# Hash attention followed by a gated feed-forward network: one pair of heads hashed together, and row loads, clears and squares moved in the order of work

## The chip, the cores and the metric

The kernel runs on one core of a Trainium2 chip. A core has a matrix engine (PE, TensorE; its weight loads are listed as PEld), a vector engine (DVE, VectorE), an activation engine (ACT, ScalarE), a general engine (POOL, GpSimd) and a queue engine (SP, SyncE), which work side by side and wait for each other by semaphores. Sixteen DMA engines move data between the chip's memory and the on-chip buffer; transfers are issued by SP, ACT or POOL. The metric is the device time of one execution in microseconds. The kernel before takes 329.41 us (median of three runs, 329.21 to 329.52).

## The reference

Attention over 4 batches, 8 heads, 768 positions of 64 values, in which a query sees only the keys of its own hash bucket, then a gated network over the 3072 rows that result.

```python
q_bits = (np.einsum('bhsd,dk->bhsk', q, proj) > 0)      # 6 bits a position, k the same
mask = q_bucket[:, :, :, None] == k_bucket[:, :, None, :]
scores = np.where(mask, scale * q @ k.T, -1e9)
attn = exp(scores - max);  attn /= (sum(attn) + 1e-9)
x = (attn @ v)  -> [3072, 512]
xn = x / sqrt(mean(x*x) + 1e-6) * rms_g
out = (silu(xn @ w_gate) * (xn @ w_val)) @ w_out        # 512 -> 1536 -> 512
```

## The kernel before, in words

**Tiling.** A batch is cut in two halves of 384 queries: `w` = 0 to 7 counts them over the batches. A *slot* is one score tile: a half `w`, a head `h` and a third `p` of the keys, two matmuls of 128 keys by 384 queries (`scores`, L355), followed by one exponential on ACT (`probs`, L365). The list `SLOTS` fixes their order. The first ones are: slots 0 to 5 are heads 0 and 1 (pair 0) for `w` = 0, slots 6 to 11 the same pair for `w` = 1, slots 12 to 17 pair 1 for `w` = 0, 18 to 23 pair 2, 24 to 29 pair 3, and from 30 on the other pairs for `w` = 1.

**Hash bits as rows.** The mask is not computed by itself. A score operand in `QK` holds the 64 values of q or k and, below them, 12 rows of hash bits, scaled so that a matmul over 76 rows gives a usable score only where all bits agree. There are six `QK` buffers, used in turn by the pairs of heads. For some pairs the matmul runs over all 128 rows instead; for them the rows below the bits must be zero (`clear_rows`, L139).

**From rows to scores.** A pair's q and k come by one load each (`load_rows`, L117, on SP). PE turns them (`turn_pe`, L181), DVE or ACT copies the result from PSUM (`keep`, L189), and POOL or ACT writes it to `QK` as 16-bit values (`cast_half`, L195 and L197). PE multiplies the turned values with the projection (`hash_bank`, L221), DVE makes bits of the signs (L228), and these are moved to their rows of `QK`. `hash_head` hashes one head, twice over, so that each block of bits has a strip of its own; three of the four blocks are then copied by DVE (L261) and one by an SP transfer (L259). `hash_heads` hashes both heads of a pair in the same four matmuls: four blocks are copied by DVE (L281) and four go by SP transfers (L279). Before, heads 2 and 3 use the first way, pairs 2 and 3 of batch 0 and the pairs of batch 1 the second.

**After the scores.** `av` (L377) multiplies the exponentials with v for a pair of heads into one PSUM tile `o_ps`, of which there is one buffer. `attn_out` empties it on DVE (`otmp`, L392, and a reciprocal, L397). `attn_x` multiplies by the reciprocal (`x`, L404) and squares (`sq`, L416), on POOL for all pairs but two; `sumsq` reduces the squares on DVE (L420). When a half's four pairs are through, `norm` makes the row scale (L427 on DVE, L429 and L433 on POOL), `scale_x` and `turn_x` make the operand of the network (L444, L458), whose matmuls (`gate` L473, `value` L483, `project` L496) are spread over the slots of the next half.

**What sets the order.** The order is written out by hand. `at(slot, function, ..., rank=)` puts a step into a slot's list, and the last loop goes through the slots: first the scores of the next slot, then the steps of rank under 3, then the exponential, then the rest by rank and by the order in which they were put. Every engine, and the DMA queues of SP and POOL, runs its own instructions in this order and waits at the first that is not ready. The loads of weights (`load_w`, L549) are issued by POOL, two halves for each of the two matrices.

The row loads of batch 1 stand in slots 9, 11 and 13 (k, q, v of pair 0) and 13, 14 and 36 (pair 1). The bits of pair 2 are moved by SP from slot 12 on.

Of the kernel before, what the change touches and what calls it, by code (L numbers as in the profile page):

```python
# [8 lines left out]
FP32 = mybir.dt.float32  # L9
# [7 lines left out]
S = 768  # L17
D = 64
# [3 lines left out]
HALF = 384  # L22
# [26 lines left out]
def kernel(  # L49
# [33 lines left out]
    pk = const.tile([128, 48], FP32, name="pk")  # L83
    pq = const.tile([128, 48], FP32, name="pq")
    thr = const.tile([128, 1], FP32, name="thr")
    scl = const.tile([128, 1], FP32, name="scl")
    mhalf = const.tile([128, 3], FP32, name="mhalf")
    gcol = const.tile([128, 4], FP32, name="gcol")
# [46 lines left out]
        if (b, hp) not in QK:  # L135
            QK[b, hp] = qkbuf[len(QK) % len(qkbuf)]

    def clear_rows(i):
        nc.gpsimd.memset(qkbuf[i][D:128].rearrange("p h n -> p (h n)").bitcast(FP32), 0.0)  # L139

    def score_rows(b, hp):
        return slice(0, 128 if (b, hp) in ((1, 0), (1, 1)) or b > 1 else KROWS)

    def t_tile(b, hp, which):
        T0[b, hp, which] = tpool.tile(
# [97 lines left out]
    def hash_head(h):  # L243


        kt, qt = t0(0, h, "k"), t0(0, h, "q")
        ps = hash_bank(
            [(pk[:, 0:32], kt), (pq[:, 0:32], qt), (pk[:, 12:44], kt), (pq[:, 12:44], qt)]
        )
        bt = bits_tile(h)  # L250
        signs(bt, ps)

        def move(movers, t0=0):
            for t, eng in enumerate(movers, t0):
                src = bt[32 * t : 32 * t + 12]
                if eng is nc.scalar:
                    nc.scalar.copy(bit_rows(0, h, t), src)
                elif eng is nc.sync:
                    eng.dma_start(out=bit_rows(0, h, t), in_=src)  # L259
                else:  # L260
                    eng.tensor_copy(bit_rows(0, h, t), src)  # L261

        return move
# [81 lines left out]
    def idle(ps, n):  # L345

        for _ in range(n):
            nc.tensor.matmul(ps, ones16, ones16, start=True, stop=True)  # L348

    def scores(g):  # L350
        w, h, p = SLOTS[g]
        ps = scps.tile([128, 2, 512], FP32, name="s_ps")
        idle(ps[:, 0, HALF:512], {0: 8, 3: 6}.get(g, 0))
        for j in range(2):
            nc.tensor.matmul(  # L355
                ps[:, j, 0:HALF], k_cols(w // 2, h, 2 * p + j), q_cols(w, h),
                start=True, stop=True,
            )
        sps[g] = ps
# [25 lines left out]
    def attn_out(w, hp):  # L385
        b = w // 2
        if w not in x:
            x[w] = xpool.tile([128, 3, DMODEL], FP32, name="x")
            ssp[w] = xpool.tile([128, 3, 4], FP32, name="ssp")
        o = ot.pop((w, hp))  # L390
        tmp = spool.tile([128, 3, 2, 66], FP32, name="otmp")
        nc.vector.tensor_add(  # L392
            tmp[:, :, :, 0:65], o[:, :, :, 0:65],
            cvb[b % 2][:, 2 * hp : 2 * hp + 2, 0:65].unsqueeze(1).to_broadcast([128, 3, 2, 65]),
        )
        r = spool.tile([128, 3, 2, 1], FP32, name="rcp")
        nc.vector.reciprocal(r, tmp[:, :, :, 64:65])  # L397
        return tmp, r

    def attn_x(w, hp, tmp, r):  # L400
        xd = x[w][:, :, 128 * hp : 128 * hp + 128]
        urgent = (w, hp) in ((0, 2), (0, 3))
        eng = nc.vector if urgent else nc.gpsimd
        eng.tensor_mul(  # L404
            xd.rearrange("p c (h d) -> p c h d", h=2), tmp[:, :, :, 0:64],
            r.to_broadcast([128, 3, 2, 64]),
        )
        sq = spool.tile([128, 3, 128], FP32, name="sq")
        if urgent:
            for c in range(3):  # L410
                nc.vector.scalar_tensor_tensor(
                    out=sq[:, c], in0=xd[:, c], scalar=1.0, in1=xd[:, c],
                    op0=ALU.mult, op1=ALU.mult, accum_out=ssp[w][:, c, hp : hp + 1],
                )
        else:
            nc.gpsimd.tensor_mul(sq, xd, xd)  # L416
        return sq
# [97 lines left out]
        load_rows(nc.sync, 0, hp, which)  # L515

    nc.vector.memset(ones16, 1.0)
    make_identity(nc, ident)
    nc.gpsimd.dma_start(out=pn[64:128], in_=proj)
    nc.vector.memset(pm, 0.0)  # L520
# [21 lines left out]
    for i in range(2):  # L542
        nc.gpsimd.memset(vls[i][:, :, :, 64:65], 1.0)
        nc.gpsimd.memset(vsum[i][:, :, 64:65], 6.0)
    clear_rows(4)
    clear_rows(5)

    def load_w(dst, src, n0, n1):
        nc.gpsimd.dma_start(  # L549
# [15 lines left out]
    def columns_of_proj():  # L565
        rows = pn.unsqueeze(1).to_broadcast([128, 4, 6])
        for t, sign in ((pk, 1.0), (pq, -1.0)):
            nc.vector.scalar_tensor_tensor(
                out=t[:, 0:24].rearrange("p (c n) -> p c n", n=6), in0=pm, scalar=sign,
                in1=rows, op0=ALU.mult, op1=ALU.mult,  # L570
            )
# [11 lines left out]
    keep(nc.scalar, 0, 0, "q")  # L583
    cast_half(0, 0, "q", 0, nc.scalar)
    columns_of_proj()
    idle(wz[:, 0:128], 5)
    bits0 = hash_head(0)
    keep(nc.scalar, 0, 1, "k")
# [23 lines left out]

    moves = {}

    def hash_one(h):
        moves[h] = hash_head(h)
        moves[h]((nc.sync,), 3)

    def hash_pair(b, hp):
        moves[b, hp] = hash_heads(b, hp)  # L620
        odd = [(0, 2), (1, 2), (0, 3), (1, 3)]
# [2 lines left out]

    for h in range(2):
        at(1 + h, cast_half, 0, h, "q", 1)
        at(h, (bits0, bits1)[h], (nc.vector,), 3)

    for hp, turns, sv in ((1, (1, 2, 3, 5), 8), (2, (7, 8, 9, 10), 17), (3, (12, 13, 14, 15), 22)):
        for i, s in enumerate(turns):  # L630
            at(s, keep_pair, 0, hp, i)
            at(s + 1, casts, 0, hp, i)
            if i % 2:
                at(s + 2, cast_half, 0, 2 * hp + i // 2, "q", 0, nc.scalar)
        at(sv, v_prep, 0, hp)

    for h, s in ((2, 4), (3, 7)):
        at(s, hash_one, h)
        for t in range(3):
            at(s + 1 + t, lambda h=h, t=t: moves[h]((nc.vector,), t), rank=5)  # L640
    for hp, s, slots in ((2, 12, (13, 14, 15, 16)), (3, 17, (18, 19, 20, 21))):
        at(s, hash_pair, 0, hp)
        for i, s in enumerate(slots):
            at(s, lambda hp=hp, i=i: moves[0, hp](nc.vector, [divmod(i, 2)]), rank=5)
    for hp, s in enumerate((6, 16, 22, 30)):
        at(s, v_mean, 0, hp, 2, range(6))
    for i, (t, src) in enumerate(((wg, moe_w_gate), (wv, moe_w_val))):
        at(2 + 4 * i, load_w, t, src, 0, 768)
        at(19 + 5 * i, load_w, t, src, 768, 1536)
        at(38 + 7 * i, load_wo, 6 * i, 6 * i + 6)  # L650

    at(78, load_grow)


    for hp, loads, turns, sh, evens, sv in (
        (0, (9, 11, 13), (20, 21, 24, 27), 33, (41, 42), (27, 44)),
        (1, (13, 14, 36), (29, 31, 33, 35), 40, (45, 47), (49, 51)),
    ):
        for which, sl in zip("kqv", loads):
            at(sl, load_rows, nc.sync, 1, hp, which)  # L660
        for i, sl in enumerate(turns):
            at(sl, keep_pair, 1, hp, i)
            at(sl + 1, casts, 1, hp, i)
        at(sh, hash_pair, 1, hp)
        for hh, sl in enumerate(evens):
            at(sl, cast_half, 1, 2 * hp + hh, "q", 0)
        at(sv[0], v_prep, 1, hp)
        at(sv[1], v_sum, 1, hp)
# [30 lines left out]
    for hp, s in enumerate((48, 62, 64, 78)):  # L699
        at(s, v_mean, 1, hp, 2)  # L700

    for i, s in ((2, 76), (3, 78), (0, 97), (1, 98)):
        at(s, clear_rows, i, rank=6)

    gts, sqs = {}, {}
# [20 lines left out]
    for w in range(8):  # L726
        for h in range(H):
            end = LAST[w, h] + (2 if (w, h) == (0, 7) else 3)
            at(end - 1, av, w, h, 0, 9)
            at(end, av, w, h, 9, 18)  # L730
            if h % 2:
                if (w, h) == (1, 1):
                    at(end, o_first, w, 0, rank=4.5)
                    at(end + 3, o_last, w, 0, rank=4.5)
                else:
                    at(end, o_step, w, h // 2, rank=4.5)
                if (w, h) not in ((0, 5), (0, 7)):
                    late = 3 if h == 7 and w < 7 else 4
                    at(end + late, s_step, w, h // 2, rank=5)
        s0 = 24 * w + 42  # L740
        n0 = {0: 11, 2: 7, 3: 13, 4: 13, 5: 13, 6: 13}.get(w, 11)
        at(s0 - n0, norm, w, rank=5)
        for c in range(3):
            scale, rank = {0: 6, 2: 6 - c}.get(w, 8 - c), 1
            turn = {0: (4, 3, 2), 2: (4, 2, 1)}.get(w, (5, 3, 1))[c]
            if w in BY_DMA and c < 2:
                scale, turn, rank = 11 - c, 11 - c, 6
            at(s0 - scale, scale_x, w, c, rank=5)
            at(s0 - turn, turn_x, w, c, rank=rank)
        seen = set()  # L750
        for ft in range(NF):
            for f, s in ((g_step, s0 + 16 * ft // NF), (v_step, s0 + (32 * ft + 16) // (2 * NF))):
                at(s, f, w, ft, rank=4 if s in seen else 2)
                seen.add(s)
        for i in range(9 if w < 7 else 6):
            c, j = divmod(i, 3)
            at(s0 + 16 + i, project, w, c, 4 * j, 4 * j + 4, rank=1 if i == 8 else 3)
# [55 lines left out]
```

## Time and profile before

| | |
|---|---|
| median of three runs | 329.41 us |
| the profiled execution's own time | 329.47 us |
| its span (first to last instruction) | 327.6 us |
| granted TensorE clock, mean | 0.998 |
| read from memory, written to it | 28.58 MB, 6.29 MB |
| SP's transfers, share of 16 DMA engines over the span | 35.2% |
| POOL's transfers, the same | 9.3% |

Rows of a timeline give the start and the time in us, the engine, the line, what is written and read, and in brackets the idle time before, with what ended it. A "q" behind an engine's name is its instruction queue, which issues transfers. The chain is the work that ended last, followed back from the last instruction.

### The profile page before, as it was taken

What the parts mean: (1) busy time and instruction counts of PE and PEld (TensorE: products, weight loads), DVE (VectorE), ACT (ScalarE), POOL (GpSimd) and SP (SyncE); (2) the same over time, 40 slices, a digit from 0 to 9 for tenths busy, and PEclk for the clock granted to TensorE, in tenths of its full rate; (3) what the DMA queues carried; (4) which work ended last, traced back from release to release, by engine and by line L of the source; (5) the groups of instructions that cost most, each with busy time, mean ns of one, the idle gap of its engine ahead of it and who ended that gap; (6) DMA issues with size and microseconds to landing.
All of it is one profiled execution on the core that took longest, in us unless ns stands there. A gap on an engine that the chain in (4) does not pass through costs nothing.

```text
span 327.6 us, 7853 instructions
## 1 busy us (share of the span) xinstructions
PE 321.5 (98%) x2975; PEld 199.5 (61%) x2975; DVE 234.9 (72%) x526; ACT 208.1 (64%) x324; POOL 165.4 (50%) x238
## 2 busy tenths in 40 slices
PE   8998999999999999999999999999999999999995
PEld 7576766655566556655566656566566656655654
DVE  4798896888598976989487865967267824793860
ACT  3788986775576666657576766667677766423331
POOL 7887977278658685686734274733221320230000
PEclk9999999999999999999999999999999999999999
DMA  7998988984359729911470814001200012002002
GB/s 216 358 212 244 165 131 154 151 179 70 119 109 172 128 48 226 155 39 26 130 128 18 150 24 152 3 18 22 78 32 2 11 24 98 0 3 96 2 0 97
DMA packets 85509, 32.69 MB, mean 100 GB/s; under 512 B 70376, under 2 KB 82400, under 8 KB 85472
## 3 DMA queue, kind: packets, MB, share of 16 engines
q1 hardware_dynamic: 81392, 27.28, 35.2%
q0 software_dynamic: 3712, 4.72, 9.3%
q8 instruction: 23, 0.38, 0.5%
q10 hardware_dynamic: 368, 0.20, 0.2%
q14 instruction: 14, 0.11, 0.1%
HBM read 28.58 MB, written 6.29 MB: 106 GB/s over the span
## 4 chain that ended last, share of the span: by engine, by line
PE 94%; DMA 2%; ACT 2%; DVE 0%; issue 0%; DVEq 0%; ACTq 0%
PE v_ps L483 19%; PE s_ps L355 19%; PE y_ps L496 18%; PE g_ps L473 15%; PE o_ps L377 10%; PE d_ps L221 4%; PE s_ps L473 4%; PE t_ps L181 2%; DMA QK<-bits 2%; ACT psb L365 1%; PE z_ps L348 1%; PE x_ps L458 1%; DMA out_dram<-ysb 1%; PE m_ps L336 1%; DVE bits L228 0%
## 5 line engine op out<-in xcount | busy, mean ns | idle before, releaser
L365 ACT ACTIVATE psb<-s_ps 128x768 f16<-128x768 f32 x192 | 150.7, 809 | 30.1 <-PE s_ps L355 28.1
L355 PE MATMUL s_ps<-QK 128*128 128x384 f16 (+1 forms) x384 | 93.7, 326 | 1.3 <-DMA QK<-bits 0.5
L483 PE MATMUL v_ps<-xnT,wv 128*128 128x384 f16 x384 | 78.1, 326 | 0.0
L496 PE MATMUL y_ps<-wo,ht 128*128 128x512 f16 x276 | 69.2, 379 | 0.0
L404 POOL TENSOR_TENSOR x<-otmp,rcp 128x384 f32<-128x384 f32 x30 | 25.7, 857 | 83.4 <-DVE rcp L397 83.2
L377 PEld LDWEIGHTS <-psb 128*128 128x128 f16 x1152 | 51.7, 98 | 21.8 <-issue 3.7
L475 ACT ACTIVATE t<-g_ps 128x384 f32<-128x384 f32 x78 | 38.2, 490 | 40.7 <-PE g_ps L473 38.2
L473 PE MATMUL g_ps<-xnT,wg 128*128 128x384 f16 x312 | 63.5, 326 | 0.0
L484 DVE SCALAR_TENSOR_TENSOR t<-t,g_ps 128x384 f32<-128x384 f32 x78 | 42.9, 550 | 28.3 <-ACT t L475 28.2
L485 DVE SCALAR_TENSOR_TENSOR ht<-t,v_ps 128x384 f16<-128x384 f32 x96 | 53.2, 554 | 11.5 <-PE v_ps L483 1.0
L377 PE MATMUL o_ps<-vl,psb 128*128 128x65 f16 x1152 | 56.0, 193 | 0.0
L483 PEld LDWEIGHTS <-wv 128*128 128x128 f16 x384 | 36.5, 98 | 22.9
L473 PEld LDWEIGHTS <-wg 128*128 128x128 f16 x384 | 36.1, 98 | 23.0
L496 PEld LDWEIGHTS <-ht 128*128 128x128 f16 x276 | 26.3, 98 | 26.5 <-issue 2.1
L355 PEld LDWEIGHTS <-QK 128*128 128x128 f16 (+1 forms) x384 | 31.1, 97 | 16.8 <-issue 3.1
L503 ACT COPY ysb<-y_ps 128x512 f32<-128x512 f32 x23 | 13.5, 585 | 24.3 <-PE y_ps L496 23.7
L392 DVE TENSOR_TENSOR otmp<-o_ps,cvb 128x390 f32<-128x390 f32 x32 | 17.9, 559 | 14.9 <-PE o_ps L377 14.8
L416 POOL TENSOR_TENSOR sq<-x 128x384 f32<-128x384 f32 x30 | 25.5, 849 | 2.4
L213 POOL CAST QK<-kT 64x768 f16<-64x768 f32 x20 | 17.0, 848 | 10.8 <-DVE kT L205 8.9
L213 POOL CAST QK<-qT 64x768 f16<-64x768 f32 x20 | 16.5, 823 | 10.8 <-DVE qT L205 8.1
L205 DVE STREAM_TRANSPOSE kT<-kL 128x192 f32<-128x192 f32 x40 | 19.7, 521 | 0.0
L205 DVE STREAM_TRANSPOSE qT<-qL 128x192 f32<-128x192 f32 x40 | 19.4, 518 | 0.0
(81 smaller groups left out, 307.2 us busy)
## 6 DMA issues: line engine op xcount, KB each, us to landing
vL<-in_v_dram SPq DMA_DIRECT2D x16, 384.0 KB
out_dram<-ysb SPq DMA_DIRECT2D x23, 256.0 KB
kL<-in_k_dram SPq DMA_DIRECT2D x40, 96.0 KB
qL<-in_q_dram SPq DMA_DIRECT2D x40, 96.0 KB
kL<-in_k_dram SPq DMA_DIRECT2D x5, 384.0 KB
qL<-in_q_dram SPq DMA_DIRECT2D x5, 384.0 KB
wg<-in_moe_w_gate_dram POOLq DMA_DIRECT2D x2, 768.0 KB, 8.5
wv<-in_moe_w_val_dram POOLq DMA_DIRECT2D x2, 768.0 KB, 9.6
```

The costliest lines, as they stand in the source:

```text
L205: nc.vector.transpose(dst.rearrange("p (c t r) -> p r c t", c=6, r=4)[:, r : r + 1], src.rearrange("p (r c) d -> p r c d", r=4)[:, r : r + 1],
L213: nc.gpsimd.tensor_copy(QK[b, hp][0:64, hh, o : o + S], T0[b, hp, which][64 * hh : 64 * hh + 64, :])
L355: nc.tensor.matmul(ps[:, j, 0:HALF], k_cols(w // 2, h, 2 * p + j), q_cols(w, h), start=True, stop=True,)
L365: nc.scalar.activation(psb[w, h][:, p], sps.pop(g)[:, :, 0:HALF], AF.Exp, scale=ESCALE,)
L377: nc.tensor.matmul(o[:, c, hh, 0:65], psb[w, h][:, jt // 2, jt % 2, 128 * c : 128 * c + 128], vls[b % 2][:, h, v_chunk(b, h, jt), 0:65], s ...
L404: eng.tensor_mul(xd.rearrange("p c (h d) -> p c h d", h=2), tmp[:, :, :, 0:64], r.to_broadcast([128, 3, 2, 64]),)
L473: nc.tensor.matmul(g, wg[:, kt, fs], xnT[w][:, kt], start=(kt == 0), stop=(kt == 3))
L475: nc.scalar.activation(t, g, AF.Tanh, scale=0.5)
L483: nc.tensor.matmul(vv, wv[:, kt, fs], xnT[w][:, kt], start=(kt == 0), stop=(kt == 3))
L484: nc.vector.scalar_tensor_tensor(out=t, in0=t, scalar=1.0, in1=g, op0=ALU.add, op1=ALU.mult)
L485: nc.vector.scalar_tensor_tensor(out=ht[w][:, ft], in0=t, scalar=0.5, in1=vv, op0=ALU.mult, op1=ALU.mult)
L496: nc.tensor.matmul(y, ht[w][:, ft, c * 128 : (c + 1) * 128], wo[:, ft, :], start=(ft == 0), stop=(ft == NF - 1),)
```

## The change

- `hash_one` is gone. Heads 2 and 3 are hashed as a pair by `hash_heads` at slot 5; the four even blocks are copied by DVE at slots 6, 7, 9 and 10, the other four go by SP. Before, head 2 was hashed at slot 4 and head 3 at slot 7.
- The turns of that pair stand at slots 1, 1, 2 and 3 (before 1, 2, 3 and 5), with their casts one slot, and ACT's casts two slots, behind.
- The last bit blocks of heads 0 and 1 are copied at slots 2 and 4, at the end of the slot.
- The six idle matmuls ahead of slot 3's scores are gone.
- Clears: POOL clears buffers 1 and 2 at the start, ACT buffer 4 (a copy of a zero column), DVE buffer 5 in two halves. Later POOL clears buffer 0 at slot 50 and 3 at slot 78 (before: 2, 3, 0 and 1 at 76, 78, 97 and 98). More pairs use all 128 rows.
- Row loads of batch 1: slots 6, 6 and 9 for pair 0, slots 9, 9 and 36 for pair 1.
- x and squares of pair 0: `attn_out` stays at the end of the pair for `w` = 0 and 1, but `attn_x` goes to slots 22 and 24 and `sumsq` to slots 24 and 26 (before: `attn_x` at slots 8 and 17, `sumsq` at 12 and 18). The reduce of pair 1 for `w` = 0 goes from slot 24 to 22. `otmp` and `rcp` get three buffers, `sq` one.
- The second halves of the gate and value weights are issued at slots 21 and 25 (before 19 and 24).
- Pair 2's even blocks are copied at slots 13, 13, 15 and 16 (before 13 to 16).

```diff
-    def clear_rows(i):
-        nc.gpsimd.memset(qkbuf[i][D:128].rearrange("p h n -> p (h n)").bitcast(FP32), 0.0)
+    def clear_rows(i, eng=nc.gpsimd, heads=(0, 1)):
+        for h in (heads if eng is nc.vector else (0,)):
+            part = qkbuf[i][D:128, h] if eng is nc.vector else (
+                qkbuf[i][D:128].rearrange("p h n -> p (h n)"))
+            part = part.bitcast(FP32)
+            if eng is nc.scalar:
+                eng.copy(part, zcol[D:128].to_broadcast([D, 2 * S]))
+            else:
+                eng.memset(part, 0.0)
 
     def score_rows(b, hp):
-        return slice(0, 128 if (b, hp) in ((1, 0), (1, 1)) or b > 1 else KROWS)
+        return slice(0, KROWS if (b, hp) in ((0, 0), (0, 3)) else 128)
...
-        idle(ps[:, 0, HALF:512], {0: 8, 3: 6}.get(g, 0))
+        idle(ps[:, 0, HALF:512], {0: 8}.get(g, 0))
...
-        tmp = spool.tile([128, 3, 2, 66], FP32, name="otmp")
+        tmp = spool.tile([128, 3, 2, 66], FP32, name="otmp", bufs=3)
...
-        sq = spool.tile([128, 3, 128], FP32, name="sq")
+        sq = spool.tile([128, 3, 128], FP32, name="sq", bufs=1)
...
-    clear_rows(4)
-    clear_rows(5)
+    clear_rows(1)
+    clear_rows(2)
+    clear_rows(4, nc.scalar)
+    clear_rows(5, nc.vector, (0,))
...
     columns_of_proj()
+    clear_rows(5, nc.vector, (1,))
...
     for h in range(2):
         at(1 + h, cast_half, 0, h, "q", 1)
-        at(h, (bits0, bits1)[h], (nc.vector,), 3)
+        at(2 + 2 * h, (bits0, bits1)[h], (nc.vector,), 3, rank=6)
 
-    for hp, turns, sv in ((1, (1, 2, 3, 5), 8), (2, (7, 8, 9, 10), 17), (3, (12, 13, 14, 15), 22)):
+    for hp, turns, sv in ((1, (1, 1, 2, 3), 8), (2, (7, 8, 9, 10), 17), (3, (12, 13, 14, 15), 22)):
...
-    for h, s in ((2, 4), (3, 7)):
-        at(s, hash_one, h)
-        for t in range(3):
-            at(s + 1 + t, lambda h=h, t=t: moves[h]((nc.vector,), t), rank=5)
-    for hp, s, slots in ((2, 12, (13, 14, 15, 16)), (3, 17, (18, 19, 20, 21))):
+    for hp, s, slots in (
+        (1, 5, (6, 7, 9, 10)), (2, 12, (13, 13, 15, 16)), (3, 17, (18, 19, 20, 21))
+    ):
         at(s, hash_pair, 0, hp)
...
-        at(19 + 5 * i, load_w, t, src, 768, 1536)
+        at(21 + 4 * i, load_w, t, src, 768, 1536)
...
-        (0, (9, 11, 13), (20, 21, 24, 27), 33, (41, 42), (27, 44)),
-        (1, (13, 14, 36), (29, 31, 33, 35), 40, (45, 47), (49, 51)),
+        (0, (6, 6, 9), (20, 21, 24, 27), 33, (41, 42), (27, 44)),
+        (1, (9, 9, 36), (29, 31, 33, 35), 40, (45, 47), (49, 51)),
...
-    for i, s in ((2, 76), (3, 78), (0, 97), (1, 98)):
+    for i, s in ((0, 50), (3, 78)):
         at(s, clear_rows, i, rank=6)
...
             if h % 2:
-                if (w, h) == (1, 1):
+                if w < 2 and h == 1:
                     at(end, o_first, w, 0, rank=4.5)
-                    at(end + 3, o_last, w, 0, rank=4.5)
+                    at(22 + 2 * w, o_last, w, 0, rank=4.5)
+                    at(24 + 2 * w, s_step, w, 0, rank=4)
                 else:
                     at(end, o_step, w, h // 2, rank=4.5)
-                if (w, h) not in ((0, 5), (0, 7)):
+                if (w, h) not in ((0, 1), (0, 5), (0, 7), (1, 1)):
                     late = 3 if h == 7 and w < 7 else 4
-                    at(end + late, s_step, w, h // 2, rank=5)
+                    if (w, h) == (0, 3):
+                        at(22, s_step, w, 1, rank=4)
+                    else:
+                        at(end + late, s_step, w, h // 2, rank=5)
```

More of the change, by code (lines that the diff above doesn't have):

```diff
@@ L85 @@
     thr = const.tile([128, 1], FP32, name="thr")
+    zcol = const.tile([128, 1], FP32, name="zcol")
     scl = const.tile([128, 1], FP32, name="scl")
@@ L395, in attn_out @@
         )
-        r = spool.tile([128, 3, 2, 1], FP32, name="rcp")
+        r = spool.tile([128, 3, 2, 1], FP32, name="rcp", bufs=3)
         nc.vector.reciprocal(r, tmp[:, :, :, 64:65])
@@ L517 @@
     nc.vector.memset(ones16, 1.0)
+    nc.vector.memset(zcol, 0.0)
     make_identity(nc, ident)
@@ L613 @@
     moves = {}
-    def hash_one(h):
-        moves[h] = hash_head(h)
-        moves[h]((nc.sync,), 3)
     def hash_pair(b, hp):
```

## The prediction, made before the result was known

> **What bounds the kernel now.** I read the page first (busy shares, then the chain that ended last), then who waited for whom on the tensor engine, then the timelines of its first 50 us, since every edit lies there.
>
> ```profile
> span 327.6 us, 7853 instructions
> PE 321.5 (98%) x2975; PEld 199.5 (61%) x2975; DVE 234.9 (72%) x526; ACT 208.1 (64%) x324; POOL 165.4 (50%) x238
> ...
> PE 94%; DMA 2%; ACT 2%; DVE 0%; issue 0%; DVEq 0%; ACTq 0%
> ```
>
> ```profile
> PE s_ps L355 <- DMA QK<-bits: 0.5, 1, 0.5
> ```
>
> TensorE (PE) is 94% of the chain, and its longest wait after the start is 0.5 us, for one transfer: its program is the time. So an edit counts for what it takes out of PE's list, or for a wait that it puts into it. The one transfer in the chain is the move of hash bits into the score operand.
>
> ```profile
> 4.01 0.85 PE L181 MATMUL t_ps<-ident,kL 128*128 128x128 f32 x3
> 4.66 0.85 PE L181 MATMUL t_ps<-ident,qL 128*128 128x128 f32 x3
> ...
> 10.97 0.50 PE L348 MATMUL s_ps<-ones 128*128 128x128 f16 x6 [0.24 <-ACT psb L365]
> 11.30 0.49 PE L355 MATMUL s_ps<-QK 76*128 76x384 f16 x2
> ...
> 20.93 0.49 PE L355 MATMUL s_ps<-QK 76*128 76x384 f16 x2
> ...
> 28.83 0.65 PE L355 MATMUL s_ps<-QK 76*128 76x384 f16 x3 [0.47 <-DMA QK<-bits]
> ...
> 30.37 0.49 PE L181 MATMUL t_ps<-ident,kL 128*128 128x128 f32 x3
> 30.70 0.44 PE L377 MATMUL o_ps<-vl,psb 128*128 128x65 f16 x9
> ...
> 36.50 0.44 PE L377 MATMUL o_ps<-vl,psb 128*128 128x65 f16 x9
> ```
>
> These are PE's own rows (start, time): two sets of transposes at the start, the six idle matmuls of slot 3, the scores of slot 13, the second half of slot 19's scores (waiting for the bits of pair 2), the last AV of pair 1 (slot 20), and the first AV of head 6 (slot 28). A slot is one score tile.
>
> **The change, part by part.**
>
> *PE work that goes.* Heads 2 and 3 were hashed one by one, and are now hashed as one pair; the six idle matmuls go.
>
> ```profile
> 13.17 1.00 PE d_ps L221 x8
> ...
> 16.81 0.78 PE d_ps L221 x8
> ...
> 22.78 0.68 DVE bits L228
> 23.48 5.21 DMA QK<-bits
> ```
>
> In the chain the hash of head 2 starts at 13.17 and that of head 3 at 16.81; one of them, 0.78 us, goes. The idle matmuls fill 10.97 to 11.30, 0.33 us, behind a wait of 0.24 us that ends earlier when a transpose stands there instead. PE gains 0.78 + 0.33 + 0.24 = 1.35 us up to slot 12.
>
> *The bits of pair 1* now go by four transfers of SP, not two; one is needed at slot 13 (before: VectorE wrote it). The pair's hash stands one slot later than head 2's did, so its bits are ready at about 13.17 + 1.00 + 0.68 and some 0.3 more, 15.2 us. Like the transfer in the chain (5.21 us) they would land at 20.4; PE, 1.35 us ahead, wants them 0.16 us into slot 13, at 20.93 + 0.16 - 1.35 = 19.7. Bounds: 0 to 0.7 us, swallowed by the next wait. Pulling the turns of pair 1 to slots 1 to 3 pulls their copies on VectorE and casts on POOL and ACT with them; on POOL it puts one cast (0.50, row at 36.28 below) ahead of the first weight load, which moves that load's 768 KB by 0.5 us behind rows that fill the DMA engines anyway: nothing.
>
> *Row loads of batch 1.* SP's program before and after differs here: k and q of batch 1's first pair stood ahead of pair 2's bits, three more (v, and k and q of the second pair) behind them. Now all five stand ahead.
>
> ```profile
> 19.26 0.46 SPq L117 DMA_DIRECT2D kL<-in_k_dram  x1
> 19.82 0.41 SPq L117 DMA_DIRECT2D qL<-in_q_dram  x1
> 23.48 3.53 SPq L279 DMA_DIRECT2D QK<-bits  x4
> ```
>
> The columns of the next rows are the stretch, the busy time of PE, PEld, DVE, ACT and POOL, the clock, the DMA share and GB/s.
>
> ```profile
> 12.00:14.00 2.00, 2.00 (x17) 0.90 (x14) 1.70 (x5) 2.00 (x4) 1.88 (x4) 1.00 1.08 383
> 20.00:22.00 2.00, 2.00 (x31) 1.52 (x33) 1.84 (x6) 2.00 (x5) 1.65 (x2) 1.00 1.16 207
> 26.00:27.00 1.00, 0.85 (x16) 0.44 (x17) 0.92 (x4) 0.98 (x2) 0.73 (x3) 1.00 0.70 224
> 27.00:28.00 1.00, 1.00 (x16) 0.38 (x17) 0.90 (x4) 0.93 (x2) 0.94 (x2) 1.00 0.17 56
> ```
>
> The 16 DMA engines are full (share over 1) until 26 us: first rows at 383 GB/s, then the two weight halves at 207. The two row loads issued at 19.26 and 19.82 don't raise the rate by 22: they queue, and the bits behind them land at 23.48 + 5.21 = 28.69, just when the engines run empty. Three more loads of 384 KB (1.18 MB) at 383 GB/s are 3.1 us. As nothing idles before, they push the bits to 31.8, and slot 19 from 28.83 to 31.9: +3.1 us. Upper bound 3.6 (slower landings); lower bound: were SP's rows served ahead of the second weight half, five loads (5.1 us) from 22 end at 27.1, plus the 2.0 us between 26.7 and 28.69, is 29.1: +0.4. I take 3.1: the 20-to-22 row shows weights first. PE, which would have been at this place at 28.36 - 1.35 = 27.0, waits 4.9 us; the 1.35 us are lost in it.
>
> *x and squares.* For head pair 0 of row blocks w=0 and w=1, POOL's multiply (x) and square ran in slots 8 and 17; now they stand behind slot 21's work, and VectorE's reduces of the squares, which wait for them, in slots 24 and 26, ahead of pair 2's otmp on VectorE's queue. That otmp empties the only o_ps bank, for which head 6's AV (slot 28) waits.
>
> ```profile
> 32.53 0.89 POOL L404 TENSOR_TENSOR x<-otmp,rcp 128x384 f32<-128x384 f32 x1 [1.60 <-DVE rcp L397]
> 33.50 0.82 POOL L416 TENSOR_TENSOR sq<-x 128x384 f32<-128x384 f32 x1
> 34.27 1.05 POOL L197 CAST QK<-kT 64x384 f16<-64x384 f32 x2
> 35.39 0.82 POOL L321 CAST vl<-vL 128x768 f16<-128x768 f32 x1
> 36.28 0.50 POOL L197 CAST QK<-qT 64x384 f16<-64x384 f32 x1
> ...
> 36.73 0.80 POOL L549 DMA_DIRECT2D wv<-in_moe_w_val_dram  x1
> ```
>
> ```profile
> 31.66 0.56 DVE L392 TENSOR_TENSOR otmp<-o_ps,cvb 128x390 f32<-128x390 f32 x1
> ...
> 34.63 0.55 DVE L420 TENSOR_REDUCE ssp<-sq 128x3 f32<-128x384 f32 x1
> 35.53 0.56 DVE L392 TENSOR_TENSOR otmp<-o_ps,cvb 128x390 f32<-128x390 f32 x1 [0.35 <-PE o_ps L377]
> ```
>
> POOL can't start this group before pair 1's otmp (slot 20). In the new order it then runs: x and square of pair 1 (1.8 with gaps, 32.53 to 34.3), the issue of a weight load (0.8), two casts (1.05), v (0.82), a cast (0.5), and now x, square, x, square (4 x 0.86 = 3.4): with gaps 8.6 us. The last four are new here, and so is the weight issue. Then a reduce (0.55) and the otmp (0.56): PE gets the bank 9.8 us after x starts. Before, x started at 32.53 and slot 28's AV ran at 36.50, 4.0 us later. In the new run x starts 3.1 us later than it could before (VectorE, no longer queued, would start it at about 32.3): 35.4; + 8.6 + 1.2 = 45.2 us. Slot 28 slips by 45.2 - 36.5 = 8.7 us, of which 3.1 is the wait at slot 19 and 5.6 the queue on POOL. Bounds of the second part: 0 (if POOL took these squares in its own idle 1.60 us and the 4.0 us sufficed) and 5.7; I take the sum of the rows.
>
> *The clock.* PE now stands still twice, for 4.9 us and, from about 39.9, for some 5 us.
>
> ```profile
> 324.00:326.00 2.00, 0.06 (x2) 0.00 (x0) 0.29 (x1) 0.00 (x0) 0.00 (x0) 1.00 0.43 131
> 326.00:327.60 1.60, 0.00 (x0) 0.00 (x0) 0.00 (x0) 0.00 (x0) 0.00 (x0) 0.70 0.02 5
> ```
>
> After its last matmul (324.06) the clock fell within 3.5 us to a mean of 0.70; at the start three transposes are 0.65 us apart, against 0.33 at 30.37. A slow stretch like the start's (1.05 us to at least 5.3) costs at most half, 2.1 us, per wait; at least 0. After the second wait VectorE's queue, not PE, sets the pace for some us, so I take 1.0 for both. [...]
>
> *Edits at nothing.* Zeros:
>
> ```profile
> 5.54 0.48 ACT L189 COPY qT<-t_ps 128x384 f32<-128x384 f32 x1 [2.94 <-PE t_ps L181]
> 4.90 0.56 DVE L189 COPY kT<-t_ps 128x384 f32<-128x384 f32 x1 [1.40 <-PE t_ps L181]
> 6.98 0.68 DVE L228 TENSOR_SCALAR bits<-d_ps,thr,scl 128x384 f16<-128x384 f32 x1 [1.34 <-PE d_ps L221]
> 3.48 2.69 POOL L139 MEMSET QK<- 64x1536 f32 x2
> ```
>
> One clear goes to ACT (1536 columns; four of its 384-column copies are 1.9 us at most) into an idle 2.94; two half clears to VectorE (at most 1.1 each, twice its copy of 0.56) into idles of 1.40 and 1.34; POOL clears two as before. If that cover fails, 0.5 us, before the waits that swallow it. POOL's later clears (four, now two) and the scores on 128 rows instead of 76 don't touch PE's pace. The weight second halves, issued two slots and one slot later, are first used at slot 50.
>
> **Sum.** Own time of the profiled run 329.47 (span 327.6 + 1.87 around it; median 329.41). 329.47 + 3.1 + 5.6 + 1.0 = 339.2.
>
> **The rivals.**
> (1) *Only POOL's queue bites*: the bits land by 27.0. Then x starts at 32.3 - 1.35 - 0.47 = 30.5, slot 28's AV at 40.3, +3.8: 333.3. Against it: full engines until 26 us.
> (2) *Only the row loads bite*: POOL gets through its group before slot 28. +3.1: 332.6. Against it: POOL's rows leave it no idle from 32.53 to 36.78.
> (3) *Faster: PE's list alone sets the end*, as it does now. Place: slots 3 to 12; price 1.35 + 0.47 = 1.8 less, 327.6. It decides if the new waits are covered, which needs bits by 27.0 and POOL's group in 4 us instead of 8.6. For it: 94% PE in the chain now.
> (4) The pair hash gains nothing because ACT (2.00 busy of 2 in 12 to 14 us) paces the slots: half of the 1.8 us of (3) stays, 328.5.
>
> **How the numbers follow.** Chances: both waits 0.60, (1) 0.18, (2) 0.10, (3) and (4) 0.08, anything else 0.04. The forecast's own range is 336.5 (rows served early: 339.2 - 2.7) to 342.4 (2.1 for the clock at each wait: 339.2 + 3.2); the range for all takes in (1) and (2): 332.2 to 342.4. A measurement of this kernel can tell 0.2%, 0.7 us. Faster 0.08, same 0.02, slower 0.90.
>
> **What would show it.** PE waits at slot 19 for QK<-bits by some 5 us, with the DMA share over 1 until about 30; VectorE's reduce of squares waits for POOL's sq by 3 us or more; PE or PEld waits for otmp at head 6's AV; granted clock under 1 after the waits; eight hash matmuls fewer and no idle matmuls in slot 3. I'm wrong if bits land under 4 us after their issue although five loads stand ahead, or if POOL's squares end before slot 26 begins.

## The result, and the profile after

The changed kernel takes 340.15 us (median of six executions, 339.47 to 341.06) against 329.5 us for the kernel before beside it: ratio 1.032, 95% interval 1.0296 to 1.0344. It is slower, as forecast, and 0.95 us above the predicted 339.2 us. The profiled execution is the one of 341.06 us, the upper end of these; its numbers stand some 0.9 us above the median.

From the page of the kernel after, the span and the chain:

```profile
span 339.2 us, 7826 instructions
...
PE 89%; DMA 6%; POOL 2%; DVE 1%; ACT 1%; issue 1%; DVEq 0%; POOLq 0%; ACTq 0%
```

Next who waited for whom on PE (us in total, times, longest), and PE's own rows at the places where it stood still; the last is the first transpose of the normalised rows, which I use as a milestone.

```profile
PE s_ps L363 <- DMA QK<-bits: 5.8, 2, 5.0
PE o_ps L385 <- DVE otmp L400: 5.0, 1, 5.0
```

```profile
21.25 0.32 PE L363 MATMUL s_ps<-QK 128*128 128x384 f16 x1 [0.76 <-DMA QK<-bits]
33.12 1.12 PE L363 MATMUL s_ps<-QK 128*128 128x384 f16 x3 [5.00 <-DMA QK<-bits]
47.29 0.67 PE L385 MATMUL o_ps<-vl,psb 128*128 128x65 f16 x9 [5.01 <-DVE otmp L400]
57.18 0.39 PE L466 MATMUL x_ps<-ident,xn 128*128 128x128 f16 x4
```

The same milestone in the timeline of the kernel before:

```profile
44.96 0.39 PE L458 MATMUL x_ps<-ident,xn 128*128 128x128 f16 x4
```

So PE's share of the chain falls from 94% to 89%, and what came in is DMA (6%, before 2%) and POOL (2%). The 14 matmuls that the change takes out (eight of a hash, six idle ones) are gone: 2961 against 2975. Two waits of 5.0 us are new: at slot 19 for the bits of pair 2, and at slot 28 for `otmp`. By 57.18 us the kernel is 12.2 us behind; the spans differ by 11.6, so all of the loss is made before that place.

The first wait, on SP's queue (the first and last row load, then the bits) and in the chain (start, time; the bits of pair 1, then those of pair 2):

```profile
19.00 0.46 SPq L118 DMA_DIRECT2D kL<-in_k_dram  x1
...
21.17 0.37 SPq L118 DMA_DIRECT2D qL<-in_q_dram  x1
23.48 10.07 SPq L287 DMA_DIRECT2D QK<-bits  x8
```

```profile
15.68 5.43 DMA QK<-bits
...
23.48 9.51 DMA QK<-bits
```

The bits are issued at 23.48 us, as before, but land 9.51 us later, at 32.99, instead of 5.21. The second wait, on POOL's and VectorE's timelines:

```profile
37.59 0.89 POOL L412 TENSOR_TENSOR x<-otmp,rcp 128x384 f32<-128x384 f32 x1 [9.38 <-DVE rcp L405]
...
43.66 0.82 POOL L424 TENSOR_TENSOR sq<-x 128x384 f32<-128x384 f32 x1
...
45.35 0.83 POOL L424 TENSOR_TENSOR sq<-x 128x384 f32<-128x384 f32 x1
```

```profile
44.52 0.56 DVE L428 TENSOR_REDUCE ssp<-sq 128x3 f32<-128x384 f32 x1 [4.08 <-POOL sq L424]
46.21 0.56 DVE L428 TENSOR_REDUCE ssp<-sq 128x3 f32<-128x384 f32 x1 [1.14 <-POOL sq L424]
46.68 0.55 DVE L400 TENSOR_TENSOR otmp<-o_ps,cvb 128x390 f32<-128x390 f32 x1
```

POOL's group runs from 37.59 to 46.18; VectorE stands 4.08 and 1.14 us before two reduces, and only then comes `otmp`. The clock, from the windows (columns as in the prediction):

```profile
30.00:32.00 2.00, 0.00 (x0) 0.00 (x0) 0.00 (x0) 0.00 (x0) 0.00 (x0) 0.52 0.35 105
...
34.00:36.00 2.00, 2.00 (x19) 1.64 (x18) 0.00 (x0) 1.67 (x3) 0.00 (x0) 0.50 0.37 59
36.00:38.00 2.00, 2.00 (x26) 1.62 (x24) 1.75 (x5) 1.16 (x3) 0.41 (x1) 0.78 0.91 143
...
48.00:50.00 2.00, 2.00 (x16) 1.59 (x15) 1.97 (x8) 0.81 (x1) 1.24 (x2) 0.50 0.99 145
```

Behind each wait TensorE runs at a granted clock of 0.50 (34 to 36 and 48 to 50 us), busy 2.00 of 2 us while it does.

### The profile page after: what moved, and what is told of

It reads as the page before. It is cut to its first block, busy times and chain, and to the rows that moved or that the text cites. A ratio compares the mean times of both kernels' runs of the same rounds, so it can differ in the third digit from the quotient of the medians.

```text
span 339.2 us, 7826 instructions
## 1 busy us (share of the span) xinstructions
PE 323.3 (95%) x2961; PEld 200.9 (59%) x2961; DVE 236.0 (70%) x526; ACT 209.9 (62%) x325; POOL 163.1 (48%) x236
## 4 chain that ended last, share of the span: by engine, by line
PE 89%; DMA 6%; POOL 2%; DVE 1%; ACT 1%; issue 1%; DVEq 0%; POOLq 0%; ACTq 0%
PE v_ps L491 18%; PE y_ps L504 18%; PE s_ps L363 17%; PE g_ps L481 15%; PE o_ps L385 10%; DMA QK<-bits 4%; PE d_ps L229 4%; PE s_ps L481 3%; PE t_ps L189 1%; PE z_ps L356 1%; PE x_ps L466 1%; DMA qL<-in_q_dram 1%; ACT psb L373 1%; DMA out_dram<-ysb 1%; POOL sq L424 0%
## 5 line engine op out<-in xcount | busy, mean ns | idle before, releaser
L363 PE MATMUL s_ps<-QK 128*128 128x384 f16 (+1 forms) x384 | 95.5, 331 | 6.5 <-DMA QK<-bits 5.8
L385 PEld LDWEIGHTS <-psb 128*128 128x128 f16 x1152 | 52.7, 99 | 27.4 <-DVE otmp L400 5.4
L385 PE MATMUL o_ps<-vl,psb 128*128 128x65 f16 x1152 | 57.0, 195 | 5.2 <-DVE otmp L400 5.0
L428 DVE TENSOR_REDUCE ssp<-sq 128x3 f32<-128x384 f32 x30 | 15.9, 531 | 5.7 <-POOL sq L424 5.7
```

The source lines that it names most:

```text
L363: nc.tensor.matmul(ps[:, j, 0:HALF], k_cols(w // 2, h, 2 * p + j), q_cols(w, h), start=True, stop=True,)
L385: nc.tensor.matmul(o[:, c, hh, 0:65], psb[w, h][:, jt // 2, jt % 2, 128 * c : 128 * c + 128], vls[b % 2][:, h, v_chunk(b, h, jt), 0:65], s ...
```

## The experiments

The theory: two waits with two causes, the row loads ahead of pair 2's bits, and the reduces of pair 0's squares ahead of pair 2's `otmp`; the slow clock is their follow-up. The rivals: one wait is only the echo of the other; the work is too long wherever it stands; the clock costs nothing. Medians, ratios to the kernel before measured beside each, and intervals:

| kernel | median us | ratio | 95% interval |
|---|---|---|---|
| e1_rows_back | 336.85 | 1.0217 | 1.0202 to 1.0232 |
| e2_x_back | 333.31 | 1.0112 | 1.0094 to 1.0129 |
| e3_both_back | 329.47 | 1.0001 | 0.9991 to 1.0010 |
| e4_fill | 338.41 | 1.0267 | 1.0250 to 1.0284 |
| e5_reduce_late | 338.38 | 1.0274 | 1.0250 to 1.0298 |
| e6_weights_later | 335.95 | 1.0189 | 1.0170 to 1.0208 |
| e7_both_back_weights | 332.58 | 1.0101 | 1.0080 to 1.0122 |
| e8_before_weights | 336.01 | 1.0205 | 1.0192 to 1.0219 |
| e9_spread | 328.96 | 0.9986 | 0.9977 to 0.9996 |
| e10_rows_alone | 330.61 | 1.0050 | 1.0035 to 1.0065 |
| e11_w19 | 330.22 | 1.0025 | 1.0010 to 1.0039 |
| e12_w17 | 329.54 | 1.0009 | 0.9997 to 1.0021 |

### Each cause taken back alone, and both

e1, from the kernel after:

```diff
-        (0, (6, 6, 9), (20, 21, 24, 27), 33, (41, 42), (27, 44)),
-        (1, (9, 9, 36), (29, 31, 33, 35), 40, (45, 47), (49, 51)),
+        (0, (9, 11, 13), (20, 21, 24, 27), 33, (41, 42), (27, 44)),
+        (1, (13, 14, 36), (29, 31, 33, 35), 40, (45, 47), (49, 51)),
```

> The changed kernel with the row loads of batch 1 back in slots 9, 11, 13 and 13, 14, 36. Theory A (two waits with two causes: the row loads delay pair 2's bits, and VectorE's reduces of pair 0's squares hold pair 2's otmp): the wait at slot 19 falls from 5.0 us to under 1, the wait for otmp before head 6's AV stays at 4 to 5.5 us, time about 335.8 us (329.5 + 5.6 + some 0.7 for the clock; 334.8 to 336.8). Rival B (the second wait is an echo of the first, because pair 1's otmp and with it POOL's group start late): both waits go, 329 to 330.5 us. Rival C (the row loads are not the cause of the first wait): the 5.0 us stay, 340 us.

e2, from the kernel after (`otmp`, `rcp` and `sq` get their old buffers as well); e3 is both edits together.

```diff
-                if w < 2 and h == 1:
+                if (w, h) == (1, 1):
                     at(end, o_first, w, 0, rank=4.5)
-                    at(22 + 2 * w, o_last, w, 0, rank=4.5)
-                    at(24 + 2 * w, s_step, w, 0, rank=4)
+                    at(end + 3, o_last, w, 0, rank=4.5)
...
-                if (w, h) not in ((0, 1), (0, 5), (0, 7), (1, 1)):
+                if (w, h) not in ((0, 5), (0, 7)):
                     late = 3 if h == 7 and w < 7 else 4
-                    if (w, h) == (0, 3):
-                        at(22, s_step, w, 1, rank=4)
-                    else:
-                        at(end + late, s_step, w, h // 2, rank=5)
+                    at(end + late, s_step, w, h // 2, rank=5)
```

> The changed kernel with x, squares and reduces of pair 0 back where they were before (and the buffers of otmp, rcp and sq too). Theory A: the wait for otmp goes, the wait at slot 19 stays at about 5 us; 329.5 + 4.3 + some 0.5 for the clock gives 334.3 us (333.3 to 335.3). Rival B (the second wait is an echo of the first): both stay, 339 us or more. Rival D (POOL's work as a whole is too long, wherever the squares stand): a wait of some us for otmp stays, 336 to 340 us.

> The changed kernel with the row loads and the squares both back: what is left of the change is the pair hash, the early turns, the clears and the later wg and wv halves. Theory A: no wait over 1 us is left after the start; the 1.35 us of PE work that the pair hash saves are partly lost again (0.4 us later start of the scores, up to 0.8 us at slot 13 for a bit block that now goes by DMA, and slot 19 waits for bits that are issued as before), 328.5 to 329.8 us. Rival E (PE's list alone sets the end): 327.6 us. Rival F (one of the parts left costs time too): over 330.5 us.

PE's timelines, first e1, then e2, then e3:

```profile
28.99 0.65 PE L363 MATMUL s_ps<-QK 128*128 128x384 f16 x3 [1.14 <-DMA QK<-bits]
42.28 0.68 PE L385 MATMUL o_ps<-vl,psb 128*128 128x65 f16 x9 [5.47 <-DVE otmp L400]
52.72 0.39 PE L466 MATMUL x_ps<-ident,xn 128*128 128x128 f16 x4
```

```profile
32.28 1.12 PE L363 MATMUL s_ps<-QK 128*128 128x384 f16 x3 [4.42 <-DMA QK<-bits]
49.57 0.39 PE L466 MATMUL x_ps<-ident,xn 128*128 128x128 f16 x4
```

```profile
20.50 0.32 PE L363 MATMUL s_ps<-QK 128*128 128x384 f16 x1 [0.88 <-DMA QK<-bits]
25.97 0.43 PE L385 MATMUL o_ps<-vl,psb 128*128 128x65 f16 x9 [0.76 <-DVE otmp L400]
28.78 0.65 PE L363 MATMUL s_ps<-QK 128*128 128x384 f16 x3 [0.73 <-DMA QK<-bits]
36.87 0.43 PE L385 MATMUL o_ps<-vl,psb 128*128 128x65 f16 x9 [0.26 <-POOL vl L329]
45.21 0.39 PE L466 MATMUL x_ps<-ident,xn 128*128 128x128 f16 x4
```

Each edit takes its own wait away and leaves the other: in e1 the `otmp` wait is still 5.47 us though slot 19 is on time, so the second wait is no echo of the first. Against e3 the row loads alone cost 333.31 - 329.47 = 3.84 us, the squares alone 336.85 - 329.47 = 7.38, both together 10.68; the sum of the two is 11.22. e2 came 1.0 us under its forecast. e1 missed its own by 1.0 us upwards, behind the wait: 5.41 us at head 6's AV (42.28 - 36.87) have become 7.51 at the milestone (52.72 - 45.21). e3 is the kernel before in time: what the pair hash saves is gone again in waits of 0.88 us at slot 13, 0.76 for pair 1's `otmp` and 0.73 at slot 19, which starts at 28.78 against 28.83 before. So the rest of the change gains nothing here, and its two moves cost all of the loss; the two alone add up to 0.54 us more than both together, and no run shows why.

### The clock by itself

```diff
-        idle(ps[:, 0, HALF:512], {0: 8}.get(g, 0))
+        idle(ps[:, 0, HALF:512], {0: 8, 19: 80, 29: 80}.get(g, 0))
```

> The changed kernel with 80 more idle matmuls (128 by 128, about 0.055 us each, 4.4 us) ahead of the scores of slot 19 and again ahead of those of slot 29, so that TensorE is busy while it would stand still. Theory A with a clock term: both causes stay, granted clock stays at 1.00 after 30 us, and the time falls by 1.0 us (x starts sooner after slot 19) and 1.4 us (the slots behind head 6's AV) to 337.7 us (337 to 338.5). If the clock costs nothing here, because VectorE and POOL pace those slots: 340.1 us. If the idle matmuls delay the work behind them: over 340.5 us.

e4's PE timeline, then two of its windows:

```profile
27.45 4.63 PE L356 MATMUL s_ps<-ones 128*128 128x128 f16 x80
31.92 0.81 PE L363 MATMUL s_ps<-QK 128*128 128x384 f16 x4
45.40 0.45 PE L385 MATMUL o_ps<-vl,psb 128*128 128x65 f16 x9 [1.02 <-DVE otmp L400]
54.11 0.39 PE L466 MATMUL x_ps<-ident,xn 128*128 128x128 f16 x4
```

```profile
30.00:32.00 2.00, 2.00 (x39) 2.00 (x37) 0.00 (x0) 0.00 (x0) 0.00 (x0) 1.00 0.19 52
46.00:48.00 2.00, 2.00 (x33) 1.50 (x30) 1.97 (x8) 1.62 (x2) 1.35 (x2) 1.00 0.79 118
```

With PE kept busy the clock stays at 1.00 in every window from 26 to 52 us, and the kernel is 1.74 us faster although it does 160 matmuls more. From head 6's AV to the milestone it takes 8.71 us (54.11 - 45.40), where the kernel after takes 9.89. The clock is a cost of its own; the time lies in the band forecast for that, 0.7 us above its middle. The idle matmuls cover not quite all of it: 1.02 us of the wait for `otmp` are left.

### Is it the place of the reduces, or POOL's work?

```diff
-                    at(24 + 2 * w, s_step, w, 0, rank=4)
+                    at(27 + 2 * w, s_step, w, 0, rank=5)
...
-        sq = spool.tile([128, 3, 128], FP32, name="sq", bufs=1)
+        sq = (spool.tile([128, HALF], FP32, name="t", bufs=3).rearrange("p (c n) -> p c n", c=3)
+              if urgent else spool.tile([128, 3, 128], FP32, name="sq", bufs=1))
```

> The changed kernel with pair 0's reduces of squares at the end of slots 27 and 29 instead of in slots 24 and 26, so that they stand behind pair 2's otmp on VectorE's queue. POOL's work and its order stay as in the changed kernel; the squares that VectorE makes itself for pairs 2 and 3 write their unused products into a buffer of their own. If what holds head 6's AV is the place of the reduces on VectorE's queue, the 5 us wait for otmp goes, and the slow clock behind it: about the time of the kernel with x and squares put back, 333.3 us (332.5 to 335). If POOL's work as a whole is too long wherever VectorE waits for it, the wait turns up some slots later, and the time stays over 337.5 us.

e5's PE timeline at the milestone, three rows of VectorE's (pair 2's `otmp`, the later of the two reduces, the norm's reduce), and its windows:

```profile
53.45 0.40 PE L467 MATMUL x_ps<-ident,xn 128*128 128x128 f16 x4 [2.36 <-DVE xn L453]
```

```profile
40.98 0.56 DVE L400 TENSOR_TENSOR otmp<-o_ps,cvb 128x390 f32<-128x390 f32 x1 [0.93 <-PE o_ps L385]
...
46.28 0.56 DVE L429 TENSOR_REDUCE ssp<-sq 128x3 f32<-128x384 f32 x1 [0.54 <-POOL sq L425]
...
51.02 0.17 DVE L436 TENSOR_REDUCE ss<-ssp 128x3 f32<-128x12 f32 x1
```

```profile
52.00:54.00 2.00, 0.55 (x14) 0.56 (x15) 2.00 (x5) 0.00 (x0) 1.85 (x4) 1.00 0.33 64
54.00:56.00 2.00, 2.00 (x20) 1.34 (x20) 1.97 (x6) 1.27 (x2) 1.91 (x3) 0.58 0.06 14
```

There is no wait for `otmp` any more: that wait was the reduces' place on VectorE's queue. But the milestone comes only 3.7 us sooner (53.45 against 57.18), because PE now waits 2.36 us for the normalised rows, from a VectorE that is busy 2.00 of 2 us there; and the clock falls behind that wait too (0.58 in 54 to 56 us). The gain is 1.77 us where 6.9 were expected of the first theory; the time lies in the band of the second. Yet VectorE waits only 0.54 us for the late squares here. From pair 2's `otmp` to the norm's reduce it works through its own list, in 10.0 us (40.98 to 51.02), in e3 in 7.3 (35.47 to 42.76). The two reduces, 1.1 us, now stand in this list, and the x and squares of pairs 2 and 3, which VectorE makes itself, take 5.3 us there, in e3 3.3; why they take longer, no run shows.

### Rows, weights, and bits

e6, from the kernel after; e7 is the same in e3, e8 in the kernel before:

```diff
-        at(2 + 4 * i, load_w, t, src, 0, 768)
-        at(21 + 4 * i, load_w, t, src, 768, 1536)
+        at((15, 20)[i], load_w, t, src, 0, 768)
+        at((26, 31)[i], load_w, t, src, 768, 1536)
```

> The changed kernel with the four halves of the gate and value weights issued at slots 15, 20, 26 and 31 instead of 2, 6, 21 and 25; the five row loads stay ahead of pair 2's bits. If the first wait comes from the transfers of weights and rows together (rows queue behind weights, bits behind rows), it needs both, and without weights in the way the five row loads are through by about 24.5 us: no wait over 1 us at slots 13 and 19, the otmp wait stays, 336 us (335 to 337.2), the time of the kernel with the row loads put back or a little less. If the row loads alone make it: still 4 us or more at slot 19 and 340 us. If the weights now collide with pair 3's bits: a wait at slot 25, over 337.5 us.

> The kernel with row loads and squares both put back, and the weights later as above. If the 1.35 us of PE work that the pair hash takes out are lost in the two waits for bits that travel beside the weights (0.88 us at slot 13 and 0.73 us at slot 19 in the kernel without this shift), those waits go and the time is 328.0 us (327.6 to 328.6), faster than the kernel before. If the tensor engine then waits for something else, such as ACT's exponentials, VectorE's otmp or the weights themselves: 329.2 us or more.

> The kernel before with the weights at the same later slots and nothing else changed: it tells how much of the run above is owed to the weights alone. Only the wait of 0.47 us at slot 19 can go: 329.0 us (328.8 to 329.4). If it falls to 328 us as well, the pair hash saves nothing.

PE's timelines of e6, e7 and e8:

```profile
29.64 1.00 PE L363 MATMUL s_ps<-QK 128*128 128x384 f16 x3 [3.14 <-DMA QK<-bits]
42.85 0.67 PE L385 MATMUL o_ps<-vl,psb 128*128 128x65 f16 x9 [4.22 <-DVE otmp L400]
```

```profile
35.39 0.50 PE L363 MATMUL s_ps<-QK 76*128 76x384 f16 x1 [2.23 <-DMA QK<-bits]
```

```profile
37.31 0.50 PE L355 MATMUL s_ps<-QK 76*128 76x384 f16 x1 [3.18 <-DMA QK<-bits]
```

All three miss in what they wait for. In e6 slot 19 still waits 3.14 us: the slot-15 half was issued at 24.82 us, while the bits were under way. The time agrees with the forecast, its mechanism does not, and the run doesn't separate rows from weights. In e7 and e8 the wait moved to slot 25, for pair 3's bits, with the clock behind it (0.50 in 36 to 40 us in e7, in 38 to 42 in e8). The kernel before alone loses 6.7 us by such a shift. With these late weights the changed order, without its two moves, is 3.4 us faster than the order before (e7 against e8), so what it is worth hangs on which transfer is late. So e10 issues all weights behind the bits of pairs 1 to 3 and leaves the five row loads ahead (from e2: slots 27 and 31, 36 and 40):

> The changed kernel with the squares put back, and the weights issued only from slot 27 on (27 and 31, second halves 36 and 40), behind the bits of pairs 1 to 3; the five row loads stay ahead of pair 2's bits. Read at slot 19: if the 5 us wait takes rows and weights together, the rows are through by about 24.5 us at 383 GB/s, the bits land by 26, and slot 19 does not wait (under 0.5 us). If the five row loads alone make the wait: 3 us or more there. What the late weights cost behind slot 42, where they are first used, is not part of the question; without such a cost the time would be 328.5 to 329.5 us.

e10's PE timeline:

```profile
27.67 0.65 PE L363 MATMUL s_ps<-QK 128*128 128x384 f16 x3 [0.48 <-DMA QK<-bits]
43.84 0.40 PE L466 MATMUL x_ps<-ident,xn 128*128 128x128 f16 x4
62.44 0.82 PE L491 MATMUL v_ps<-xnT,wv 128*128 128x384 f16 x4 [1.66 <-DMA wv<-in_moe_w_val_dram]
```

The same five row loads ahead of the same bits now cost a wait of 0.48 us instead of 4.42 in e2. It takes rows and weights together. The bits land at 27.5 us (21.96 and 5.58 in the chain), 1.5 us later than e10's forecast had them, so the wait is only just small. And the saving of the pair hash and the idle matmuls is to be seen: the milestone comes at 43.84, 1.1 us before that of the kernel before, with the first scores at the same time (8.36 and 8.37). The second half of the value weights, 1.66 us late at 62 us, takes it away.

### Versions meant to beat both

e9: from e3, first weight halves at slots 7 and 14, second at 27 and 31, row loads at (9, 11, 18) and (18, 19, 36). e11 and e12: from e10, weights at 19 and 23 (27 and 31), and at 17 and 21 (25 and 30).

> The kernel with row loads and squares both put back, and its transfers spread: first weight halves at slots 7 and 14 (not 2 and 6), second halves at 27 and 31, row loads of batch 1 at 9, 11, 18 and 18, 19, 36, so that no weight half is issued ahead of the bits of pairs 1 and 3 by less than some 3 us. If the pair hash's saving is hidden only by late bits, all of these come in time and the time is 328.2 us (327.6 to 328.8). If bits still meet a weight half (pair 3's at slot 25, in the run with all weights later), a wait over 1 us comes there and the time is 330 us or more. If another engine paces these slots: 329.0 to 329.6 us.

> The kernel with the five row loads ahead, the squares put back and late weights, its weights pulled forward to slots 19 and 23 (second halves 27 and 31), into POOL's idle 2.3 us before pair 1's x and behind the issue of pair 3's bits. In that kernel the first transposes of the normalised rows ran 35.5 us after the first scores, against 36.6 us before, and the 1.7 us wait for the late value weights took the gain away again. If it was only the weights' lateness, the wait at 62 us goes and the time is 328.3 us (327.9 to 328.8), below the kernel before. If pair 3's bits or the next row loads now travel beside the weights: a wait of 1 to 2 us at slot 25 and the clock behind it, 330 us or more.

> The same with the weights at slots 17 and 21 (second halves 25 and 30), so that the first half is issued at about 27 us beside pair 3's bits, which slot 25 needs at about 33 us. A transfer of bits took 5.2 to 5.8 us beside weights so far, so they should land at 32 to 33 us: no wait or one under 0.5 us, and the same 328.3 us. If bits queue behind the weight half (over 6 us), a wait over 1 us at slot 25 and 330 us or more.

PE's waits in e9, then slot 19 in e11 and in e12:

```profile
PE o_ps L385 <- DVE otmp L400: 1.6, 3, 0.6
```

```profile
28.69 0.65 PE L363 MATMUL s_ps<-QK 128*128 128x384 f16 x3 [1.43 <-DMA QK<-bits]
```

```profile
28.39 0.65 PE L363 MATMUL s_ps<-QK 128*128 128x384 f16 x3 [1.29 <-DMA QK<-bits]
```

e9 has no wait for bits left and is the fastest kernel here, 328.96 us, 0.14% under the kernel before (the interval excludes 1, if narrowly, and the step is below the 0.2% that I called measurable). It lies 0.8 us over its forecast: 1.6 us of waits for `otmp`, in three places, have taken the place of those for bits. In e11 and e12 no weights stand before 27 us, as in e10, yet slot 19 waits 1.4 and 1.3 us: without weights the five row loads cost a wait of 0.5 to 1.4 us. Both miss their 328.3 us, and neither beats the kernel before. The row loads were slower in these two (268 and 208 GB/s in 22 to 24 us, in e10 326); why stays open.

## Why the prediction was right

Direction, size and mechanism held; both waits stand at the predicted places, with the predicted releasers, and last 5.0 us each (4.9 and some 5 forecast). The one term that was clearly off is the clock.

- **Row loads, 3.1 us.** Measured 3.50 at slot 19 (32.28 in e2 against 28.78 in e3), within the bounds of 0.4 and 3.6; by the medians of the same two kernels it is 2.98 (3.84 less the 0.86 of the clock below). The price by bytes at 383 GB/s holds within this scatter, and the engines moved 391 GB/s between 28 and 30 us. e10 shows its condition, the weight halves in front, which the prediction read off one window. In the profiled run of the kernel after it is 4.29 (33.12 against 28.83), of which the late start of that execution is a part (first scores at 8.76 us; in the kernels with the same beginning 7.91 to 8.71).
- **POOL's queue, 5.6 us.** Measured 5.41 (e1 against e3), and POOL's group takes 8.59 us where 8.6 were summed from rows. That it was VectorE's queue that passed the delay on to PE is shown by e5. What the step left out: with the reduces out of the way little is gained, as VectorE's own list then reaches the norm late.
- **The clock, 1.0 us.** This term was mis-sized. e4 gives 1.74 us. The failed step is "after the second wait VectorE's queue, not PE, sets the pace": behind the wait PE is busy 2.00 of 2 us at 0.50, and in e1, which has that wait alone, 2.1 us are lost between head 6's AV and the milestone (7.51 - 5.41), the bound of 2.1 in full. Behind the first wait it is 0.86 (in e2, 4.36 at the milestone less 3.50 at slot 19); there the reciprocal that pair 1's x waits for starts 4.12 us after slot 19 (at 36.40), in e3 3.26 (at 32.04). The two make 2.96, so the term lies between 1.7 and 3.0; the profiles behind the upper figure are single executions. In the profiled run of the kernel after the clock is at 0.52 in 30 to 32 us, 0.50 from there to 36, 0.78 in 36 to 38 and 1.00 in 38 to 40, with PE at work again from 33.12: it stays low for 2.9 to 4.9 us of work. With 1.0 us for both waits the sum was 0.95 too low.
- **PE work that goes, 1.35 us, lost in the waits.** Right: in e3 nothing of it is left, and with the bits out of the way (e10) 1.1 us are.
- **Bits of pair 1, 0 to 0.7 us.** 0.76 in the kernel after and 0.88 in e3: just over the bound. They landed at 21.1 us, as 15.68 + 5.43 in the chain, 0.7 later than worked out. It was swallowed, as said.
- **Clears, at nothing.** Nothing speaks against it: e3 has all of them, and its first scores start at 7.91 us, before at 8.37; but the spread of 0.8 us between kernels of the same beginning would hide a cost of the 0.5 us allowed. The scores on 128 rows took PE 326 ns each, those on 76 rows 325 (both in the kernel before).

Of the rivals, (1) and (2) are e1 and e2, kernels with one cause each: 336.85 and 333.31 against 333.3 and 332.6. Rival (1) was 3.5 us too low: it took off the 1.8 us of (3), which do not appear, and left out the clock. Rivals (3) and (4) fail by e3: without both causes the kernel is neither at 327.6 nor at 328.5 but at 329.47, and it waits 2.4 us for bits and `otmp`, but for ACT only 0.5, in the kernel before 0.7.

## What to carry to other kernels

What a small transfer cost the engine that waits for it was set here by what is queued ahead of it and what travels beside it (the wait for pair 2's bits behind the same five row loads: 4.42 us in e2, 0.48 in e10 with the weights later): before a load is moved, look at the window in which it will run and at what else is issued there, and reckon with the wait turning up at the next such transfer (2.23 us in e7, 3.18 in e8). A step moved later on POOL was paid on VectorE's queue, which stood 4.08 and 1.14 us for it ahead of the `otmp` that PE needed; moving that wait back in the queue gave 1.8 us of the 6.9 expected here, because the next consumer then waited for the same engine. And a wait of 4.4 or 5.5 us on TensorE cost 0.9 or 2.1 more behind it, at a granted clock of 0.51 (e2) and 0.50 (e1).

## What was not expected of the hardware

The clock fell for shorter waits than I thought: the prediction read a fall within 3.5 us of standing still. In e7 PE stood still for 2.23 us, after 4 us in which it was busy a good half of the time; e7's windows:

```profile
30.00:32.00 2.00, 1.03 (x14) 0.77 (x12) 1.89 (x5) 1.51 (x2) 0.62 (x1) 1.00 1.06 210
32.00:34.00 2.00, 1.16 (x21) 0.77 (x20) 1.50 (x5) 0.81 (x1) 1.69 (x3) 1.00 1.11 230
34.00:36.00 2.00, 0.61 (x3) 0.52 (x4) 0.00 (x0) 0.07 (x1) 1.81 (x5) 0.53 1.23 217
```

At 34 us it had waited 0.8 us, and the mean of the next 2 us is already 0.53. In e2 PE stood still from 27.86 us, and the clock is whole until 32 (0.51 in the next 2 us):

```profile
30.00:32.00 2.00, 0.00 (x0) 0.00 (x0) 0.48 (x2) 0.00 (x0) 0.00 (x0) 1.00 0.15 38
```

In e5 the clock fell only after PE had started again (53.45; 1.00 in 52 to 54, 0.58 in 54 to 56). In these three runs the moment isn't tied to the length of the wait alone; what ties it, they don't show. The bits of pair 1 took 5.43 us to land in the kernel after and those of pair 2, four blocks as well, 9.51, and a later place of the four weight halves cost the kernel before 6.7 us (e8): here the price of a place in the transfers was set by the neighbours, not by the size.
